# Two range checks moved from the second products to the middle pairs of first products

## The chip, the cores and the metric

The kernel runs on one core of one Trainium2 chip. The metric is the device time of one execution in microseconds (us); the median of several runs is given. The engines are TensorE (PE; its weight loads are shown apart as PEld), VectorE (DVE), ScalarE (ACT), GpSimd (POOL) and SyncE (SP). SP and POOL also issue DMA transfers, each in the order of its own queue.

## The reference

Hash attention, followed by an MLP mixer. With B=4, 8 heads, S=768 and head width 64:

```
bucket(q), bucket(k) = signs of q@proj, k@proj as 6-bit numbers
scores = where(bucket(q) == bucket(k), q@k.T / 8, -1e9); scores -= rowmax
attn   = exp(scores);  x = (attn / (sum(attn) + 1e-9)) @ v        # heads side by side: (4, 768, 512)
h      = relu(x.T @ w_tok1) @ w_tok2;   u = x + h.T                # over tokens, 768 -> 256 -> 768
out    = u + relu(u @ w_ch1) @ w_ch2                               # over channels, 512 -> 1536 -> 512
```

All inputs are float32.

## The kernel before

The work comes in three stages: attention (to about 310 us), token mixing (to about 387 us) and channel mixing, the function `channels` (the rest). The change lies in `channels` alone.

The attention stage takes exponentials without subtracting a row's maximum. This is safe while no element of q or k exceeds 1.7 in size. So, while the channels are mixed, the kernel reads q and k once more and tests them: the *range check*. There are 32 tiles to test (16 head pairs, q and k), each of 128 x 768 floats (384 KB). If any element was too large, a second, careful version of everything runs at the end; with these inputs it doesn't.

One check is spread over two functions. `begin_look` (L1554) squares the oldest fetched tile in place on ScalarE (L1556). `end_look` (L1558) takes Relu of the square minus 1.7 squared, with a sum along the row, on ScalarE (L1564), and then has POOL fetch the next tile into the place that has come free (L1574). There are three places, called `looked` (one) and `seen` (two). So the first three calls only fetch; after that each call tests the tile fetched three calls earlier; and the last three calls only test. That makes 35 calls for 32 tiles. `look` (L1547) does both halves at once.

`channels` works on three groups of 1024 tokens, s = 0, 1, 2. A group has a *first product*, u @ w_ch1 with relu, and a *second product*, the result @ w_ch2. Both are done by Strassen's scheme with seven block products, p1 to p7, instead of eight.

- First product: six blocks of hidden rows. In group 0 each is done by itself (`hidden`). In groups 1 and 2 they are done in three pairs: `hidden_first` (t = 0), and `hidden_pair` for t = 1, the *middle pair*, and t = 2. Most of their block products are themselves split by Strassen's scheme (class `Smaller`: `one`, `rest` and `three` are its matmul groups, `unite` its ScalarE copy at L988, `keep` the copy at L954). `open_next` begins the next pair's p1. The pre-added left operands are fetched on SP's queue (`fetch_hidden_left`, L873, shown as `WC<-hidden_left` or `SW<-hidden_left`).
- Second product: `outputs` (L1458). It does p1 undivided (`whole_product`, L1368) and then calls `product` (L1381) for p5, p7, p6, p3, p2 and p4. Each of these six is a *part* of the second product, split once more into seven matmul groups of six matmuls (L783) that accumulate in PSUM blocks a0, a1, b0, b1. Between them ScalarE copies blocks (L789): a0 to c1, c1 to b0, b1 to c7, a0 to a1, a0 to u, b0 to the output, a1 to c5. The last matmul group accumulates in a1, so it must wait until c5 is copied. Finished blocks of the output are added into DRAM by POOL transfers (`store`, L1468), which share POOL's queue with the fetches of the checks.

Everything is issued in the order in which it is written (the schedule is manual), and each engine works through its own list in that order. Waits between engines follow from which tile an instruction reads and writes.

Where the checks stand before the change:

- `outputs(s)`: s + 1 calls of `look` in the whole product for s = 0 and 1 (L1482), ahead of the copy of p1's result to `q1` (L1484); none for s = 2.
- `product`: two checks in each of the six parts for s = 0 and 1 (`looks = 2`, L1396), none for s = 2. The first check begins after the copy of a0 to c1 and ends after the copy to u; the second begins after the copy of b0 to the output and ends after the copy of a1 to c5.
- `hidden_first`: two; `hidden_pair`: one, in its middle (L1170).

In numbers: 13 calls in group 0, 18 in group 1, 4 in group 2.

Of the kernel before, what the change touches and what calls it, by code (L numbers as in the profile page):

```python
# [48 lines left out]
def kernel(  # L49
# [15 lines left out]
    B, NP, _, _, S = qk.shape  # L65
# [689 lines left out]
    def channels(pool, psum, SW1, second, TA, judge):  # L755
# [7 lines left out]
        last = B * S // (2 * TT) - 1  # L763
# [274 lines left out]
        def open_next(bank, s, t):  # L1038
            p1 = Smaller(None, "p1", s, t + 1)
            p1.pair = bank_pair(bank)  # L1040
            p1.one(p1.pair, left_at(7 * s + 1)[:, 2 * TT : 4 * TT])
            ahead.append(p1)
# [4 lines left out]
        def fill(t, slot):  # L1047

            for work in slots.pop((t, slot), []):
                work()  # L1050
# [70 lines left out]
        def hidden_pair(s, t):  # L1121

            r, (p2, p6, p7, p3, p4) = parts_of(s, t)
            p5, p1 = Smaller(None, "p5", s, t), ahead.pop()
            one, two, three, four = ring
            e2, e4, e5, e3 = [flat(output_at(i)) for i in ((0, 2, 2, 0) if t == 1 else (0, 1, 2, 3))]  # L1130
            e6 = e7 = flat(q1)
            before = postponed.pop() if postponed else None

            A = p1.pair
            if before:
                before[0]()
            B = bank_pair(two)
            p6.one(B, e6)
            if before:
                before[1]()  # L1140
            p1.rest()
            p1.unite()
            C = bank_pair(three)
            p2.one(C, e2)
            p1.add(True)
            p6.rest()
            p6.unite()
            p1.seed()
            p6.add(True)
            fill(t, "p6")  # L1150
            p2.rest()
            p2.unite()
            p6.seed()
            D = bank_pair(four)
            p7.one(D, e7)
            p2.add()
            p1.three(A)
            if t + 1 == GP:
                fetch_left(7 * s + 1)
            first = copies()  # L1160
            copy_pair(first, A)
            fill(t, "p2")
            p6.three(B)
            C = bank_pair(three)
            p5.one(C, e5)
            u = copies()
            plus(u, flat(B), first)
            p2.three(A)
            fill(t, "u")
            look()  # L1170
            plus(r[0], banks(A), rows(e2))
            p5.rest()
            p5.unite()
            B = bank_pair(two)
            p3.one(B, e3)
            p5.add()
            relu(r[0])
            p7.rest()
            plus(flat(C), e5, u)
            p7.unite()  # L1180
            p7.add(True)
            p3.rest()
            p3.unite()
            A = bank_pair(one)
            p4.one(A, e4)
            p7.seed()
            p5.three(C)
            p3.add()
            fill(t, "p3")
            v = copies()  # L1190
            copy_pair(v, C)
            p4.rest()
            p4.finish()
            p7.three(D)
            plus(r[3], banks(D), rows(v))
            fill(t, "end")
            p3.three(C)

            def direct():
                p4.three(D)  # L1200
                if t + 1 < GP:
                    plus(r[1], banks(C), rows(e3))

            def end():
                plus(e4, e4, u)
                plus(r[2], banks(D), rows(e4))

            if t + 1 < GP:
                later(t + 1, "p3", *bounds(r))
                later(t + 1, "end", lambda: relu(r[3]), lambda: relu(r[2]))  # L1210
                open_next(two, s, t)
                ring[:] = [two, three, one, four]
                postponed.append((direct, end))
            else:
                plus(r[1], banks(C), rows(e3))
                unfinished.append(lambda: (relu(r[3]), [work() for work in bounds(r)]))
                ring[:] = [two, one, three, four]
                postponed.append((direct, lambda: (end(), relu(r[2]))))
# [94 lines left out]
        def left_at(g):  # L1313
            return area(g % 2)[:, : 7 * QC * P]
# [66 lines left out]
        def product(s, j, name, q, early, late, final=None):  # L1381

            half = slice(0, TT // 2)
            A, B = blocks(2)
            a0, a1, b0, b1 = (pair[:, i, half] for pair in (A, B) for i in range(2))  # L1390
            w = left_at(7 * s + j).rearrange("p (i k c) -> p i k c", i=7, k=QC)
            b00, b01, b10, b11 = quarters(name)
            t2 = begun.pop()
            c1, c7, u, c5 = (a[:, i] for a in [split4(copies())] for i in range(4))
            qs = q.rearrange("p i (n t) -> p (i n) t", n=2)
            looks = 2 if s < last else 0  # L1396

            def part(ps, left, right, start=False):
                accumulate(ps, lambda k: w[:, LEFTS.index(left), k], lambda k: right[:, k], range(QC), start)

            part(a0, 4, b00, True)
            copy(a0, c1)
            if looks > 1:
                begin_look()
            part(b1, 1, extra(), True)
            copy(c1, b0)
            copy(b1, c7)
            part(a0, 2, t2)
            for work in early[:2]:
                work()  # L1410
            nc.vector.tensor_tensor(b00, b10, t2, op=ALU.subtract)
            for work in early[2:]:
                work()
            if final:
                plus(qs[:, 3], qs[:, 3], c7)
            part(b0, 5, b10)
            if j < 6:
                fetch_left(7 * s + j + 2, [0])
            copy(a0, a1)
            copy(a0, u)  # L1420
            if looks > 1:
                end_look()
            part(a1, 0, b01)
            if final:
                plus(qs[:, 0], b0, qs[:, 0])
            else:
                copy(b0, qs[:, 0])
            if looks:
                begin_look()
            part(b1, 6, b00)  # L1430
            copy(a1, c5)
            if looks:
                end_look()
            part(a1, 3, b11)
            if j < 6:
                fetch_left(7 * s + j + 2, [1])
            for work in late:
                work()
            if j < 6:
                begin(ORDER[j + 1])  # L1440
            if not final:
                plus(qs[:, 3], c7, c5)
                plus(qs[:, 2], b1, u)
                copy(a1, qs[:, 1])
                return
            plus(qs[:, 2], qs[:, 2], u)
            plus(qs[:, 3], qs[:, 3], c5)
            plus(qs[:, 2], b1, qs[:, 2])
            plus(qs[:, 1], a1, qs[:, 1])
            if j < 6:  # L1450
                nc.sync.dma_start(out=final(0), in_=q[:, 0])
                for i in range(2):
                    nc.sync.dma_start(out=final(1, i, 1), in_=qs[:, 2 + i])
                return
            for i, issuer in zip((0, 3, 2, 1), (nc.sync, nc.sync, nc.scalar, nc.sync)):
                issuer.dma_start(out=final(i // 2, i % 2, 1), in_=qs[:, i])

        def outputs(s):  # L1458
# [20 lines left out]
            if postponed:  # L1479
                postponed.pop()[1]()  # L1480
            combine("x", "r3", ALU.subtract, "r1", [(0, 0), (1, 0), (1, 1)])
            for _ in range(s + 1 if s < last else 0):  # L1482
                look()
            nc.scalar.copy(q1, ps)  # L1484
            q7, q57, q6, q5 = [output_at(i) for i in range(4)]
# [68 lines left out]
        def begin_look():  # L1554
            if due():
                nc.scalar.activation(seen[0][0], seen[0][0], ACT.Square)  # L1556

        def end_look():  # L1558

            if judge and not places:  # L1560
                places.append(pool.tile([P, 2, S], F32, name="seen", tag="seen", bufs=1))
            if due():
                t, n, i = seen.pop(0)
                nc.scalar.activation(  # L1564
                    t, t, ACT.Relu, bias=minus_safe, accum_out=excess[:, 2 * n + i : 2 * n + i + 1],
                )
            if unseen:
                n, i = unseen.pop(0)
                at = (2 * n + i) % 3
                if at == 0:  # L1570
                    t = pool.tile([P, S], F32, name="looked", tag="looked", bufs=1)
                else:
                    t = places[0][:, at - 1]
                nc.gpsimd.dma_start(out=t, in_=qk[pairs[n][0], pairs[n][1], :, i])  # L1574
                seen.append((t, n, i))
# [167 lines left out]
```

## Time and profile before

| what | us |
|---|---|
| median of 3 runs | 789.79 |
| lowest, highest | 789.23, 790.72 |
| the profiled execution | 791.4 |
| its span, from first to last instruction | 789.6 |
| TensorE busy | 782.3 (99%) |
| VectorE busy | 665.1 (84%) |
| ScalarE busy | 478.1 (61%) |
| GpSimd busy | 53.7 (7%) |
| ScalarE, Square of one tile (L1556), median of 32 | 0.847 |
| ScalarE, Relu of one tile (L1564), median of 32 | 0.937 |
| ScalarE, reading out the row sum (L1564), median of 32 | 0.19 |
| fetch of one tile (L1574), issue to landing, least, median, most | 3.5, 6.1, 10.8 |

How to read a row of the timeline: the start in us from the span's start, the duration in us, the engine, the line, the operation, `out<-in` by the program's tile names, the shapes, how many instructions are merged (x6), and in brackets the idle time of the engine before it with what ended that idle time. In a row of the list of waits: who waited, for whom, the total in us, how often, and the longest. A matmul's end is modelled and overlaps the next one's start, so distances between starts are the better measure. A row of several matmuls that runs without a break has equal distances.

### The profile page before, as it was taken

To read this page: it belongs to the slowest core of one execution; us is meant where nothing else is said; L and a number is where in the kernel's file an instruction comes from. 1 tells how busy PE (TensorE), PEld (TensorE's weight loads), DVE (VectorE), ACT (ScalarE), POOL (GpSimd) and SP (SyncE) were. 2 spreads that over 40 slices of the span, in tenths; PEclk is the share of its full clock that TensorE was granted. 3 is DMA by queue.
4 is the path that set the end of the run, shared out by engine and by line. 5 is a ranking of instruction groups with operands and counts; after the bars stand their busy time and mean duration, and the time that the engine had idled before them with its cause. 6 is when DMAs were issued, how large, how long until landed. Compare 5 with 4: busy or idle time off the path is not lost.

```text
span 789.6 us, 12604 instructions
## 1 busy us (share of the span) xinstructions
PE 782.3 (99%) x4745; PEld 480.2 (61%) x4745; DVE 665.1 (84%) x906; ACT 478.1 (61%) x825; POOL 53.7 (7%) x77
## 2 busy tenths in 40 slices
PE   9999999999999999999999999999999999999997
PEld 5444444444444444455544458868876887886886
DVE  5989898989887677999697889878899798889884
ACT  6688888888888887333323235655676665654331
POOL 1000000000000000011121010220001122000001
PEclk9999999999999999999999999999999999999999
DMA  4435353537352424795686996897766696650555
GB/s 164 164 123 164 123 164 123 164 123 244 135 178 91 136 76 160 203 272 125 113 272 210 329 376 243 250 295 206 232 187 211 246 244 159 192 154 2 184 173 127
DMA packets 102016, 144.85 MB, mean 183 GB/s; under 512 B 30200, under 2 KB 71616, under 8 KB 101952
## 3 DMA queue, kind: packets, MB, share of 16 engines
q1 hardware_dynamic: 93936, 119.15, 46.1%
q0 software_dynamic: 7728, 24.64, 13.4%
q8 instruction: 38, 0.62, 0.3%
q10 hardware_dynamic: 288, 0.21, 0.1%
q14 instruction: 26, 0.21, 0.1%
HBM read 101.01 MB, written 35.52 MB: 173 GB/s over the span
## 4 chain that ended last, share of the span: by engine, by line
PE 88%; issue 5%; DVE 2%; DMA 2%; ACT 1%; POOL 1%; SPq 0%; POOLq 0%; DVEq 0%
PE b L783 40%; PE sc L356 20%; PE acc L410 16%; PE t L656 5%; PE t L696 5%; PE sums L434 2%; DMA looked<-in_qk 1%; PE hp L301 1%; POOL seen L1574 0%; DVE R L1021 0%; DMA hidden_left<-WC 0%; PE idle L473 0%; PE hw L325 0%; DVE R L832 0%; SPq L1284 0%
## 5 line engine op out<-in xcount | busy, mean ns | idle before, releaser
L363 ACT ACTIVATE e<-sc 128x768 f32<-128x768 f32 x192 | 154.5, 811 | 6.4 <-PE sc L356 6.0
L356 PE MATMUL sc<-qk 64*128 64x384 f32 x768 | 152.9, 484 | 0.0
L783 PE MATMUL b<-R,second 128*128 128x256 f32 (+1 forms) x522 | 132.5, 409 | 1.0 <-ACT c L789 1.0
L410 PE MATMUL acc<-e,vn 128*32 128x384 f32 x1536 | 127.0, 486 | 0.0
L783 PEld LDWEIGHTS b<-R,second 128*128 128x128 f32 x522 | 98.8, 190 | 30.5 <-issue 16.5
L395 DVE TENSOR_TENSOR esd<-esd,e 128x768 f32<-128x768 f32 x96 | 92.0, 958 | 10.4 <-ACT e L363 0.5
L410 PEld LDWEIGHTS acc<-e,vn 128*32 128x32 f32 x1536 | 49.9, 110 | 73.9 <-issue 73.5
L356 PEld LDWEIGHTS sc<-qk 64*128 64x128 f32 x768 | 68.3, 188 | 42.2 <-issue 37.8
L789 ACT COPY c<-b 128x256 f32<-128x256 f32 (+1 forms) x96 | 40.2, 426 | 78.7 <-PE b L783 68.2
L783 PE MATMUL b<-XT,WC 128*128 128x256 f32 (+1 forms) x212 | 65.0, 443 | 0.0
L356 PE MATMUL sc<-bits 64*128 64x384 bf16 x384 | 62.6, 323 | 0.0
L783 PEld LDWEIGHTS b<-XT,WC 128*128 128x128 f32 x212 | 40.3, 190 | 19.8 <-issue 15.5
L391 DVE SCALAR_TENSOR_TENSOR esd<-e 128x768 f32<-128x768 f32 x32 | 30.6, 955 | 23.3 <-ACT e L363 23.3
L783 PE MATMUL b<-XT,SW 128*128 128x256 f32 (+1 forms) x164 | 47.0, 410 | 0.0
L656 PE MATMUL t<-x,W 128*128 128x512 f32 x96 | 41.8, 593 | 0.0
L356 PEld LDWEIGHTS <-bits 64*128 64x128 bf16 x384 | 18.5, 94 | 33.1 <-issue 9.7
L783 PEld LDWEIGHTS b<-XT,SW 128*128 128x128 f32 x164 | 31.1, 190 | 9.4 <-issue 4.1
L416 ACT ACTIVATE num<-acc,vsum 128x384 f32<-128x384 f32 x32 | 18.6, 582 | 29.7 <-PE acc L410 29.3
L716 POOL DMA_DIRECT2D XT<-second x8 | 9.9, 1235 | 383.3 <-DVE second L715 361.1
L455 ACT COPY rec<-rec 32x384 f32<-32x384 f32 x64 | 32.7, 510 | 5.0 <-DVE rec L449 4.2
L783 PE MATMUL b<-TA,WC 128*128 128x256 f32 (+1 forms) x92 | 33.3, 472 | 0.0
L398 DVE TENSOR_TENSOR esd<-esd,e 128x768 f32<-128x768 f32 x32 | 30.5, 954 | 1.9
(253 smaller groups left out, 1251.1 us busy)
## 6 DMA issues: line engine op xcount, KB each, us to landing
second<-left SPq DMA_DIRECT2D x20, 768.0 KB
raw<-in_moe_w_ch SPq DMA_DIRECT2D x16, 768.0 KB
qk<-in_qk SPq DMA_DIRECT2D x15, 768.0 KB
second<-left SPq DMA_DIRECT2D x18, 576.0 KB
seen<-in_qk POOLq DMA_DIRECT2D x21, 384.0 KB, 6.3
WC<-hidden_left SPq DMA_DIRECT2D x18, 448.0 KB
vn<-in_v SPq DMA_DIRECT2D x16, 384.0 KB
vt<-in_vT SPq DMA_DIRECT2D x16, 384.0 KB
```

Source lines behind the costliest of these rows:

```text
L356: nc.tensor.matmul(sc[:, i, :HALF], t[rows, 1, P * c : P * c + P], t[rows, 0, qs], start=start, stop=not start,)
L363: nc.scalar.activation(e, sc[:, :, :HALF], ACT.Exp, scale=SCALE)
L391: nc.vector.scalar_tensor_tensor(self.d, es[0], NR * EPS, es[1], op0=ALU.add, op1=ALU.add,)
L395: nc.vector.tensor_tensor(self.d, self.d, e, op=ALU.add)
L398: nc.vector.tensor_tensor(self.d, self.d, self.es[-1], op=ALU.add)
L410: nc.tensor.matmul(acc[D * i + d : D * i + d + 32], vn[:, i, c, d : d + 32], e[:, i], start=(c == 0), stop=(c == NR - 1),)
L416: nc.scalar.activation(nums[self.n][:, self.half], acc, ACT.Identity, scale=-1.0, bias=vsum,)
L455: nc.scalar.copy(rec[other : other + 32, h], rec[at : at + 32, h])
L656: nc.tensor.matmul(ps, W1[:, r, P * j : P * j + P], x[:, r], start=(r == 0), stop=(r == NR - 1),)
L696: nc.tensor.matmul(ps[at], left, right, start=start, stop=True, skip_group_check=True,)
L783: nc.tensor.matmul(ps, left(k), right(k), start=start and k == ks[0], stop=stop and k == ks[-1], skip_group_check=True,)
L789: nc.scalar.copy(c, ps)
```

## The change

The number of calls stays at 35. One check is taken out of group 0's part p4 (the first of its two), and one of the two in group 1's whole product is taken out. One check is added to the middle pair (t = 1) of group 1 and of group 2: its Square stands ahead of p3's `three`, its Relu and its fetch stand behind `open_next`. Groups 0, 1 and 2 then have 12, 18 and 5 calls.

```diff
@@ hidden_pair
             p7.three(D)
             plus(r[3], banks(D), rows(v))
             fill(t, "end")
+            if t == 1:
+                begin_look()
             p3.three(C)
@@ hidden_pair
                 later(t + 1, "p3", *bounds(r))
                 later(t + 1, "end", lambda: relu(r[3]), lambda: relu(r[2]))
                 open_next(two, s, t)
+                if t == 1:
+                    end_look()
                 ring[:] = [two, three, one, four]
                 postponed.append((direct, end))
@@ product
-            looks = 2 if s < last else 0
+            looks = 0 if s == last else 1 if s == 0 and j == 6 else 2
@@ outputs
             combine("x", "r3", ALU.subtract, "r1", [(0, 0), (1, 0), (1, 1)])
-            for _ in range(s + 1 if s < last else 0):
+            if s < last:
                 look()
             nc.scalar.copy(q1, ps)
```

## The prediction

> **What bounds the kernel now.** I read the page first, then the list of waits, then the timelines of TensorE (PE), ScalarE (ACT), GpSimd (POOL) around the two waits found, and last the timeline of ACT where the change puts its new work.
>
> The page's head and the list of waits for TensorE over the whole span:
>
> ```profile
> span 789.6 us, 12604 instructions
> PE 782.3 (99%) x4745; PEld 480.2 (61%) x4745; DVE 665.1 (84%) x906; ACT 478.1 (61%) x825; POOL 53.7 (7%) x77
> PE b L783 <- ACT c L789: 1.5, 2, 1.0
> PE idle L473 <- DVE ones L97: 1.1, 1, 1.1
> ```
>
> TensorE is the bound: it is idle for 7.3 us of 789.6, part of it before the first and after the last matmul. Between its matmuls only two waits are listed, 1.5 us together, both in the channel mixing that the change touches and both for a ScalarE copy (L789). So the most that moving ScalarE work can give is these two and the slow restarts behind them. The timelines of TensorE around them:
>
> ```profile
> 519.07 4.05 PE L783 MATMUL b<-R,second 128*128 128x256 f32 x18
> 524.07 1.56 PE L783 MATMUL b<-R,second 128*128 128x256 f32 x6 [0.96 <-ACT c L789]
> 525.47 1.02 PE L783 MATMUL b<-XT,WC 128*128 128x512 f32 x2
> ...
> 601.37 1.46 PE L783 MATMUL b<-second,second 128*128 128x256 f32 x6
> 603.33 1.56 PE L783 MATMUL b<-c,second 128*128 128x256 f32 x6 [0.50 <-ACT c L789]
> 604.75 1.56 PE L783 MATMUL b<-R,second 128*128 128x256 f32 x6
> ```
>
> The idle times in brackets understate the loss, because a matmul's end is modelled. From starts: a part of 6 matmuls undisturbed takes 1.30 us (the two parts before 519.07 start at 516.48 and 517.77), 0.216 each. Stall A: 18 from 519.07 should be followed at 522.96; the next starts at 524.07, 1.11 late, and then takes 1.40 to the row after instead of 1.30: 1.21 us. Stall B: the part due at 602.67 starts at 603.33, 0.66 late; it takes 1.42 instead of 1.30, and the next lasts 1.56 instead of 1.46: 0.88 us. Together 2.09 us.
>
> ScalarE in stall A (group 0's last part, p4) and the POOL queue that feeds it:
>
> ```profile
> 516.95 0.85 ACT L1556 ACTIVATE seen<-seen 128x768 f32<-128x768 f32 x1
> 519.92 0.94 ACT L1564 ACTIVATE seen<-seen,minus_safe 128x768 f32<-128x768 f32 x1
> 520.85 0.36 ACT L789 COPY second<-b 128x256 f32<-128x256 f32 x1
> 522.92 0.84 ACT L1556 ACTIVATE looked<-looked 128x768 f32<-128x768 f32 x1 [1.70 <-DMA looked<-in_qk]
> 523.67 0.35 ACT L789 COPY c<-b 128x256 f32<-128x256 f32 x1
> ...
> 512.10 0.95 POOL L1574 DMA_DIRECT2D looked<-in_qk  x1
> ```
>
> The check that the change removes here is the one at 516.95/519.92. It does not itself wait: its Square sits in a gap before the next copy. What waits is the second check, at 522.92, for its tile, fetched at 512.10 and landed 10.8 us later; the copy of c5 (523.67) is queued behind it, and TensorE's last part behind that.
>
> ScalarE in stall B (group 1's whole product):
>
> ```profile
> 598.42 0.83 ACT L1556 ACTIVATE seen<-seen 128x768 f32<-128x768 f32 x1
> 600.22 0.83 ACT L1556 ACTIVATE looked<-looked 128x768 f32<-128x768 f32 x1
> 602.02 0.99 ACT L1484 COPY q<-b 128x1024 f32<-128x1024 f32 x1
> 602.91 0.37 ACT L789 COPY c<-b 128x256 f32<-128x256 f32 x1
> ```
>
> No transfer is late here: two checks of 1.80 us each run back to back, behind a relu that VectorE (DVE) released at 597.46, and the two copies come after them.
>
> ScalarE at the place of the new checks, end of group 1's middle pair:
>
> ```profile
> 565.18 1.06 ACT L1027 ACTIVATE R<-R 128x1024 f32<-128x1024 f32 x1
> 567.94 0.37 ACT L954 COPY second<-b 128x256 f32<-128x256 f32 x1 [1.69 <-PE b L783]
> 569.74 0.37 ACT L954 COPY q<-b 128x256 f32<-128x256 f32 x1 [1.43 <-PE b L783]
> ```
>
> Two holes, 1.69 and 1.43 us, both ended by TensorE. Group 2's middle pair has the same two (1.69 before 698.03, 1.44 before 699.84).
>
> **What the skill says.** The Trainium skill, "ScalarE: Activation LUTs", section "What ACT_TABLE_LOAD costs", prices an ACTIVATE at 186 ns + 0.833 ns per element, 280 with a pointer bias, and says neighbours overlap by 93 ns: 826 and 920 ns for 768 elements. The trace has 847 and 937, and 0.19 for reading the sum; I use the trace. "DMA: Bandwidth & Descriptors", "Anatomy of one DMA — SWDGE (gpsimd) path", gives 2.0 us + bytes/436e3, 2.9 us for a tile of 393,216 bytes. The trace shows 3.5 at best, 6.1 in the median, 10.8 at worst, so the queueing, not the price, makes stall A. The same page ("Issuing engines are not separate DMA queues") says that transfers of all issuers interleave on the same engines; the trace agrees, DMA share being 0.95 from 456 to 481 and 1.09 from 524 to 540 us.
>
> **The change part by part.** A call squares the tile fetched three calls earlier, then fetches into its place. I number calls and fetches from 1; before, group 0 has calls 1 to 13, its p4 calls 12 and 13.
>
> 1. *Removed in group 0's p4: one Square, one Relu with its read, one POOL fetch.* ScalarE work: 0.85 + 1.03 (0.94 + 0.19 - 0.09 overlap), hidden where it stood, worth nothing alone. But the remaining call becomes number 12 and takes fetch 9, issued at 505.29 and landed at 514.40, instead of fetch 10 (landed 522.89). Then: b0's copy goes at about 520.6 (its part ends at 520.5), Square at 520.9 to 521.7, c5's copy at about 521.9, when its matmuls are through, done by 522.3; TensorE wants it at 522.96. Margin 0.7 us. Stall A goes: -1.21.
> 2. *What moves with it.* POOL issues one tile fewer between 522 and 531; fetch 12 then stands behind the store issued at 522.13 (free at 523.4), as before. Fetch 13 waits behind the next store (531.41) and is needed only at about 566. In group 1's first stage call 13 takes fetch 10 (landed 522.89, wanted about 524.7) and call 14 fetch 11 (landed 523.95); before, its second Square stood 1.50 us for fetch 12 until 532.32, covered by TensorE's work. TensorE arrives 1.2 us earlier at the hidden-left tiles that SP fetched: they landed at 523.07 to 534.57, and the first is used at 528.9 (later 527.7), 4.6 us after landing; the others have more. No new wait: 0.
> 3. *Added at the end of the middle pair, groups 1 and 2: Square ahead of p3's three, Relu and read behind the next pair's opening.* Square 0.85 goes in the 1.69 hole (566.14 to 567.0, spare 0.9), Relu and read 1.03 in the 1.43 hole (spare 0.4). Their tiles landed long before. Behind them on ScalarE is the copy of p6's first product, which TensorE's next parts wait for; without the hole each pair would cost 1.88. I take 0, between 0 and that. The holes end on TensorE, so nothing is gained either.
> 4. *The fetch added there.* POOL is free (busy 0.00 from 564 to 571). In group 1 it puts 0.39 MB on the DMA engines from about 569 (share 0.51 from 564 to 571). The hidden-left tiles in flight landed at 572.45 and 573.93, and TensorE's sequencer first asks at 577.9 and 580.9: 5.4 us spare, against 1.6 us for 0.39 MB at the 246 GB/s that the stretch 480 to 524 moved. In group 2 all 32 tiles are fetched by then, so no fetch at all. 0.
> 5. *Removed in group 1's whole product: 1.80 us of ScalarE and a fetch.* q1's copy can start at about 600.3 (the product's last wide matmul starts at 599.64 and takes 0.59), c1's copy at about 601.5 when its own part ends, done at 601.9; TensorE wants it at 602.67. Margin 0.7. Stall B goes: -0.88; only 0.88 of the 1.80, because TensorE's work covers the rest. The next calls use tiles fetched one place earlier, so the 0.19 wait at 607.07 falls too, off the path.
> 6. *Untouched:* group 1's last part keeps three calls between fetch and use, and its small loss at 653.85 (0.2 us; Square waits 0.68 for its tile).
>
> Sum -1.21 - 0.88 = -2.1 us. The profiled execution took 791.4 (span 789.6 plus 1.8 around it) and would take 789.3; it is 1.6 above the median of the runs, so I take the 2.1 off the median: 789.79 - 2.1 = **787.7 us**, 0.27%. About 0.2%, or 1.58 us, is what a measurement of this kernel can tell from no change (faster below 788.2, slower above 791.4).
>
> **Rivals.**
> - *Only A pays.* B's wait is replaced: q1's copy or VectorE, without a gap from 577 to 607, sets the next part. For it: ScalarE's relu waits for VectorE until 597.46. Against: 0.7 us margin, and b00 (VectorE, 604.37) is wanted at about 606.6. 789.79 - 1.21 = 788.6.
> - *Only B pays, or neither.* The DMA queue is late again for another consumer after A, such as call 13's tile, 1.8 us before use. 788.9, or 789.8.
> - *Slower: the checks in the middle pairs hold ScalarE.* If the holes were not there for them, p6's first copy would be 1.88 late in each pair and TensorE with it: 3.76 - 2.09 = +1.7, 791.5. It becomes slower than before from 1.05 us per pair, past 0.2% from 1.84. Against: the holes exceed the work by 0.9 and 0.4.
> - *The change removes a check that did not wait* and so does nothing for A (788.9): step 1 speaks against it; it holds only if the remaining Square still needs fetch 10.
>
> **How the numbers follow.** Forecast 0.72 (787.0 to 788.2 by itself: jitter of the transfers, and 653.85's loss going or growing). Only A 0.10; only B 0.04; neither 0.04; slower 0.10, of which 0.06 the middle pairs and 0.04 a late transfer that I don't see. Range 786.9 to 788.9: forecast and both halves, 0.86. Faster 0.72, same 0.18, slower 0.10.
>
> **What would show it.** Right: TensorE's list of waits has no L789 entry over 0.1 us at these places; the only Square in group 0's p4 starts about 1 us before c5's copy without waiting; q1's copy starts right after one check; both holes of the middle pairs are filled and the copies after them still end on TensorE. Wrong: a Square waiting for a transfer in group 1's first stage, an idle TensorE at the start of a last pair, or TensorE's busy time growing by as much as its idle time falls.

## The result

The changed kernel takes 788.99 us in the median (788.29 to 790.5, 22 runs), the kernel before 790.15 on the same chip (789.23 to 791.2, 22 runs): ratio 0.9986, 95% interval 0.9980 to 0.9993, so -1.1 us, between -0.55 and -1.6. The forecast was -2.1 us and 787.7, with a range up to 788.9. The direction was right; the size was about half, and the time lies just outside the range.

The page's head of the profile after, and TensorE's list of waits over the whole span:

```profile
span 787.9 us, 12602 instructions
PE 781.7 (99%) x4745; PEld 480.9 (61%) x4745; DVE 664.8 (84%) x906; ACT 478.1 (61%) x825; POOL 53.9 (7%) x77
PE idle L473 <- DVE ones L97: 1.1, 1, 1.1
PE b L783 <- ACT c L789: 0.4, 1, 0.4
```

Of the two listed waits for L789 one entry of 0.4 us remains, and it is neither of the two. TensorE's timeline of after at the three places:

```profile
514.48 2.86 PE L783 MATMUL b<-R,second 128*128 128x256 f32 x12 [0.42 <-ACT c L789]
519.76 5.34 PE L783 MATMUL b<-R,second 128*128 128x256 f32 x24
524.95 1.88 PE L783 MATMUL b<-XT,WC 128*128 128x512 f32 x4
...
600.84 1.46 PE L783 MATMUL b<-second,second 128*128 128x256 f32 x6
602.13 1.24 PE L783 MATMUL b<-c,second 128*128 128x256 f32 x5
```

Group 0's last 24 matmuls run in one row (18 and 6 before, with stall A between them), and the part at 602.13 follows 1.29 us after 600.84: both stalls are gone. The 0.42 at 514.48 is in group 0's part p2, ahead of everything that was changed; there ScalarE waited 1.16 us for fetch 8 (fetches are numbered as in the prediction). ScalarE in group 0's p4, the whole product and the middle pair of group 1, in after (lines have moved by four: L1560 is the Square, L1568 the Relu, L1488 the copy to q1):

```profile
521.53 0.85 ACT L1560 ACTIVATE seen<-seen 128x768 f32<-128x768 f32 x1
522.55 0.37 ACT L789 COPY c<-b 128x256 f32<-128x256 f32 x1 [0.18 <-PE b L783]
...
599.74 1.02 ACT L1488 COPY q<-b 128x1024 f32<-128x1024 f32 x1
601.04 0.37 ACT L789 COPY c<-b 128x256 f32<-128x256 f32 x1 [0.28 <-PE b L783]
...
565.61 0.83 ACT L1560 ACTIVATE looked<-looked 128x768 f32<-128x768 f32 x1
567.41 0.37 ACT L954 COPY second<-b 128x256 f32<-128x256 f32 x1 [0.96 <-PE b L783]
567.68 0.94 ACT L1568 ACTIVATE looked<-looked,minus_safe 128x768 f32<-128x768 f32 x1
569.15 0.37 ACT L954 COPY q<-b 128x256 f32<-128x256 f32 x1 [0.45 <-PE b L783]
```

The Square in p4 doesn't wait, and the copies at 522.55, 601.04, 567.41 and 569.15 are all ended by TensorE: in all four places ScalarE now waits for TensorE and not the other way round. So the mechanism came out as forecast, and so nearly did the profiled execution: 791.4 before, 789.78 after, 789.3 forecast. What fell short is the median, 788.99.

### The profile page after: what moved, and what is told of

It is laid out like the page before. It is cut to its first block, busy times and chain, and to the rows that moved or that the text cites. A ratio compares the mean times of both kernels' runs of the same rounds, so it can differ in the third digit from the quotient of the medians.

```text
span 787.9 us, 12602 instructions
## 1 busy us (share of the span) xinstructions
PE 781.7 (99%) x4745; PEld 480.9 (61%) x4745; DVE 664.8 (84%) x906; ACT 478.1 (61%) x825; POOL 53.9 (7%) x77
## 4 chain that ended last, share of the span: by engine, by line
PE 92%; issue 4%; DVE 2%; DMA 1%; POOL 0%; ACT 0%; POOLq 0%; DVEq 0%
PE b L783 43%; PE sc L356 20%; PE acc L410 16%; PE t L656 5%; PE t L696 5%; PE sums L434 2%; DMA seen<-in_qk 1%; PE hp L301 1%; PE idle L473 0%; PE hw L325 0%; POOL seen L1578 0%; DVE R L832 0%; DVE TA L1364 0%; POOL looked L1578 0%; DVE R L1357 0%
## 5 line engine op out<-in xcount | busy, mean ns | idle before, releaser
L395 DVE TENSOR_TENSOR esd<-esd,e 128x768 f32<-128x768 f32 x96 | 92.0, 958 | 10.4 <-ACT e L363 0.5
L789 ACT COPY c<-b 128x256 f32<-128x256 f32 (+1 forms) x96 | 40.2, 425 | 79.2 <-PE b L783 68.9
```

Of the source, the lines that this page charges most:

```text
L395: nc.vector.tensor_tensor(self.d, self.d, e, op=ALU.add)
L789: nc.scalar.copy(c, ps)
```

## The experiments

Two theories. **Theory 1**: the profile of before showed an unusual execution. B is ScalarE's own work and in every execution; A depends on when a transfer lands (fetch 10, the tile that p4's second check squares), and is small or absent in many. **Theory 2**: both stalls are in every execution with the profile's sizes, and about 1 us is lost again elsewhere.

### The kernel before, profiled again, and each half alone

Unchanged, with 21 runs:

> The kernel before, unchanged, profiled once more. Theory 1 (the profiled execution of before was an unusual one: stall A comes from a transfer that is as late as 10.8 us only now and then, stall B from ScalarE's own work and so in every execution): stall B is there again with 0.85 to 0.9 us, stall A is well below 1.2 us, between 0 and 0.7, and the span is below 789.6. Theory 2 (both stalls are in every execution with the sizes of the first profile, and the change loses about 1 us elsewhere): A 1.1 to 1.3 and B 0.85 to 0.9 us again. Time: ratio 1.000 under both, within 0.001.

Measured: ratio 0.9998 (0.9992 to 1.0005), profiled execution 790.86. TensorE around p4 of group 0:

```profile
518.31 4.05 PE L783 MATMUL b<-R,second 128*128 128x256 f32 x18
523.36 1.56 PE L783 MATMUL b<-R,second 128*128 128x256 f32 x6 [1.00 <-ACT c L789]
524.76 0.59 PE L783 MATMUL b<-XT,WC 128*128 128x512 f32 x1
```

Counted as in the prediction, A is 1.26 us (due at 522.20, plus 0.10), B 0.87. This is what theory 2 expected, and against theory 1's number. Fetch 10 took 10.7 us.

The first half alone (shortened, against the kernel before):

```diff
-            looks = 2 if s < last else 0
+            looks = 0 if s == last else 1 if s == 0 and j == 6 else 2
+            if t == 1 and s == 1: begin_look()   # ahead of p3.three(C)
+                if t == 1 and s == 1: end_look() # behind open_next
```

> Only the first half of the change: the first check of group 0's part p4 goes to the middle pair of group 1; the whole product of group 1 keeps two checks. Theory 1 (stall A is small in most executions): -0.2 to -0.5 us, ratio 0.9994 to 0.9998. Theory 2 (A has 1.2 us in every execution): -1.2 us, 0.9985, or if the new place of the check costs time, more than that is lost again and TensorE shows a wait at the start of group 1's last pair. In its profile: no wait for a transfer in group 0's p4, stall B as before, 0.85 to 0.9 us.

Measured: 789.77 against 790.38 (65 runs), ratio 0.9992 (0.9986 to 0.9999): -0.6 us, between -0.1 and -1.1, about half of A. In its profile TensorE has no wait in p4, B is 0.87, and TensorE doesn't wait at the start of the last pair. So nothing was lost at the new place in this execution.

The second half alone (shortened, against the kernel before):

```diff
-            for _ in range(s + 1 if s < last else 0):
+            if s < last:
                 look()
+            if t == 1 and s == last: begin_look()
+                if t == 1 and s == last: end_look()
```

> Only the second half: one of the two checks of group 1's whole product goes to the middle pair of group 2. Theory 1 (B is made by ScalarE's own work and falls in every execution): -0.9 us, ratio 0.9989. Theory 2 (both stalls in every execution, part of the gain lost at the new places): -0.9 us or less. A rival under which B gives nothing in the end, because VectorE or the copy of q1 sets the next part: 0, ratio 1.000. In its profile: no L789 wait of TensorE near 602 us, group 0's p4 as before with a stall A of any size.

Measured: 789.32, ratio 0.9989 (0.9982 to 0.9995): -0.9 by the ratio and -1.1 by the medians; B's 0.88 lies inside the interval. And its profile, with p4 of group 0 just as before the change, shows no A at all:

```profile
519.14 5.34 PE L783 MATMUL b<-R,second 128*128 128x256 f32 x24
524.32 1.02 PE L783 MATMUL b<-XT,WC 128*128 128x512 f32 x2
PE idle L473 <- DVE ones L97: 1.1, 1, 1.1
```

Here fetch 10 took 9.1 us. The same code gives 1.2 us in one execution and nothing in another.

### No late transfers

The kernel before, with the fetches of the checks left out after the first three. 29 of the 32 tiles are therefore never read, and the tests run on the first three (shortened; the edit also keeps one `looked` tile for all its calls):

```diff
-                nc.gpsimd.dma_start(out=t, in_=qk[...])
+                if 2 * n + i < 3:
+                    nc.gpsimd.dma_start(out=t, in_=qk[...])
```

> The kernel before with the fetches of the checks left out after the first three: Squares and Relus run as often, on tiles that are already there, so 29 of the 32 tiles are not read at all. No check can then wait for its transfer, and the DMA engines have 11 MB less to move; stall B stays. Theory 1: all that late transfers cost in a usual execution (group 0's parts p2 and p4, group 1's p4) is 0.3 to 0.8 us: ratio 0.9990 to 0.9996. Theory 2: 1.2 us in group 0's p4 alone, 1.5 us or more in all: 0.9981 or less.

Measured: 789.71 (789.38 to 790.33, 13 runs), ratio 0.9992 (0.9984 to 1.0000). In its profile B is there with 0.87 and nothing else of this kind. So all that late tiles cost in a usual execution is about 0.7 us, between 0 and 1.3. Theory 2 wanted 1.5 us or more; its 0.9981 lies outside the interval (A's 1.2 us alone, 0.9985, would still lie inside). The runs also lie closer together: 0.95 us from least to most in 13 runs, against 2.5 over the 65 of before.

### How often is A there?

> The kernel before, unchanged, a third profile. So far stall A had 1.2 us in two profiles of before, with fetch 10 landing 10.7 and 10.8 us after its issue, and none at all in the profile of only_b, whose code is the same up to there and whose fetch 10 took 9.1. If A comes and goes with the transfer: anything from 0 to 1.3 us, by fetch 10's time less about 9.5 us, and B 0.86 again. If A belongs to the kernel and only_b's profile was the odd one: 1.2 us again.

> The kernel before, unchanged, a fourth profile. As for the third: A between 0 and 1.3 us by fetch 10's time less about 9.5 us if it comes and goes; 1.2 us if it belongs to the kernel.

Measured: 789.64 in the third profiled execution, 791.11 in the fourth. TensorE in the third, then in the fourth:

```profile
518.79 5.34 PE L783 MATMUL b<-R,second 128*128 128x256 f32 x24
523.97 1.45 PE L783 MATMUL b<-XT,WC 128*128 128x512 f32 x3
601.82 1.56 PE L783 MATMUL b<-c,second 128*128 128x256 f32 x6 [0.50 <-ACT c L789]
```

```profile
519.25 4.05 PE L783 MATMUL b<-R,second 128*128 128x256 f32 x18
524.13 1.13 PE L783 MATMUL b<-R,second 128*128 128x256 f32 x4 [0.83 <-ACT c L789]
```

A is 0 in the third and 1.09 in the fourth (due at 523.14, plus 0.10); B is there in both. Together with the experiment below, which came out with the same order of instructions, six profiles have the same code up to this place: A was 1.21, 1.26, 1.09, 0, 0 and 0, with fetch 10 at 10.8, 10.7, 10.5, 8.8, 9.1 and 9.1 us. Where it is there, A is within 0.1 us of fetch 10's time less 9.5 us, as expected. The mean is 0.6, the gain of the first half alone. Six profiles are few for a mean, but the spread of the runs points the same way: the 21 runs of the first half alone lie within 1.2 us (789.0 to 790.21), those of the second half alone, which keeps A, within 3.8 (788.39 to 792.18).

### What makes fetch 10 late?

Two attempts on five other transfers, the hidden-left tiles for group 1 (448 KB each), which SP issues from 511.7 us on, right after the store that POOL issues ahead of fetch 10 (511.20). The first put four of them at the end of p4's code instead of p2's:

```diff
-        *([lambda h=h: fetch_hidden_left(h) for h in range(5)] ...)      # end of p2
+        *([lambda: fetch_hidden_left(0)] ...)                            # end of p2
+        *([lambda h=h: fetch_hidden_left(h) for h in range(1, 5)] ...)   # end of p4
```

> The kernel before, with four of the five transfers of 448 KB that fetch group 1's first hidden-left tiles issued on SP's queue at the end of group 0's p4 instead of the end of its p2; the checks are not touched. If fetch 10 is late because it shares the DMA engines with these five: it lands within 9 us of its issue, stall A is 0 in this profile, B stays at 0.86, and the time falls by what A costs in the mean, 0.4 to 0.8 us (ratio 0.9990 to 0.9995). If fetch 10 is late for another reason, such as the store that POOL issued just ahead of it: still over 9.5 us, A up to 1.2, ratio 1.000. A loss is possible if the four tiles now come too late for group 1's first stage: a wait of TensorE between 528 and 545 us.

Measured: ratio 1.0004 (0.9996 to 1.0012). The edit did nothing: SP has nothing else to do between these two places and waits for nothing there, so its list is the same, and it issued the tiles at 511.78 and on as before. The run serves only as one more execution of before (A was 0, as counted above).

The second attempt issues them one by one behind SP's waits, at the ends of p5, p7, p6, p3 and p2:

> The kernel before, with the five transfers of 448 KB for group 1's first hidden-left tiles issued one by one, each at the end of one of group 0's parts p5, p7, p6, p3 and p2, instead of all five in a row behind p2's last fetch; the checks are as before. SP waits for TensorE's progress at each part, so they really go out about 9 us apart from 490 us on, while the DMA share is 0.64 (496 to 503) and not 0.95 to 1.1 (512 to 524). If fetch 10 is late because these five crowd in with the store just ahead of it: it takes under 8 us instead of 8.8 to 10.8, stall A is 0, B stays at 0.86, and the time falls by A's mean, 0.5 to 0.8 us (ratio 0.9990 to 0.9994). If the store itself is slow: fetch 10 still over 8.8, ratio 1.000.

Measured: ratio 1.0004 (0.9996 to 1.0013). SP now issues four of the five before 506 us, but the last, and a transfer of 256 KB that stood behind them (L881, at 524.91 in the first profile), now go out right behind the store:

```profile
510.11 1.25 POOL L1468 DMA_DIRECT2D out<-TB  x1 [5.02 <-DVE XT L859]
510.97 0.43 SPq L873 DMA_DIRECT2D SW<-hidden_left  x1
511.44 1.42 SPq L881 DMA_DIRECT2D SW<-hidden_left  x1
```

From the store's issue to its landing the DMA engines moved 329 GB/s (510.11 to 519.82), against 294 in the first profile of before (511.20 to 521.82), so the edit did not make room for it. The store took 9.7 us, fetch 10 landed 1.05 us after it and took 9.5; A was 0.10. The time did not fall. In this one profile the losses turned up elsewhere:

```profile
599.35 1.46 PE L783 MATMUL b<-second,second 128*128 128x256 f32 x6
601.66 1.56 PE L783 MATMUL b<-c,second 128*128 128x256 f32 x6 [0.85 <-ACT c L789]
653.12 1.56 PE L783 MATMUL b<-R,second 128*128 128x256 f32 x6 [0.57 <-ACT c L789]
```

B has 1.2 us here, and group 1's p4 0.8 (653.12). Whether that is usual of this kernel one profile can't say. Moving four of the five transfers away doesn't make the fetch quick, but a store with nothing else beside it was not tried; what makes the fetch 9 or 10.7 us stays open.

### The change again, and taken further

> The changed kernel, unchanged, timed and profiled again. If A was there in about half of before's executions (3 of 6 profiles with the same code up to that place: 1.2, 1.3, 1.1, 0, 0, 0) and B in all: -0.6 - 0.88 = -1.5 us, ratio 0.9981, less what p2's check loses by chance. If the first measurement was right as it stood: 0.9986. If the forecast's sizes hold after all: 0.9973. In its profile: no L789 wait near p4 of group 0 nor at 602; in p2 of group 0 between 0 and 0.7 us.

Measured: 789.09 against 790.23, ratio 0.9986 (0.9980 to 0.9993), the same as the first time; the 0.9981 worked out from the six profiles is in the interval too. In its profile fetch 10 took 10.8 us, as late as in any execution, and yet nothing waits for it. ScalarE in p4, and the list of waits:

```profile
520.97 0.85 ACT L1560 ACTIVATE seen<-seen 128x768 f32<-128x768 f32 x1
521.99 0.37 ACT L789 COPY c<-b 128x256 f32<-128x256 f32 x1 [0.18 <-PE b L783]
PE idle L473 <- DVE ones L97: 1.1, 1, 1.1
```

This shows step 1 of the prediction directly: the late tile is no longer the one that p4 needs.

What was left in the changed kernel is p2 of group 0, where a Square waits for fetch 8 (TensorE loses 0.68 us in one profile of the change, 0.25 in the other). In p4 of group 1 neither profile of the change loses anything, but three others did (0.2, 0.4 and 0.8 us). So the same move was made in both parts, with the checks put into `hidden_first` (shortened):

```diff
-            looks = 0 if s == last else 1 if s == 0 and j == 6 else 2
+            looks = 0 if s == last else 1 if j == 6 or s == 0 and j == 5 else 2
@@ hidden_first
             copy_pair(u, X)
+            begin_look()
@@ hidden_first
             p7.one(bank_pair(x), e7)
+            end_look()
```

> The changed kernel taken further: group 0's part p2 also has one check instead of two, and so has group 1's p4; the two checks taken out go to the first stage of groups 1 and 2, Square behind the copy of p6's block to u, Relu and fetch behind the opening of p7. So the checks in p2 and p4 of group 0 and in p4 of group 1 each have more time for their fetch. If late transfers in these three parts are what is left: no wait of TensorE for L789 anywhere in the second products, and a gain over before of the change's 1.2 to 1.5 us plus 0.3 to 0.5, ratio 0.9976 to 0.9981. If the gains are given back at the new places: no faster than the change, 0.9986, and waits of TensorE in the first stages.

> The changed kernel taken further (one check in p2 and in p4 of group 0 and in p4 of group 1, the others in group 1's and 2's first stage) together with the five hidden-left transfers spread over group 0's parts. The first alone had no stall left in the second products. If nothing else waits for these transfers: the same as without the spread, 0.9977 within 0.0008. If the quieter DMA engines help elsewhere: up to 0.3 us better.

Measured: 788.76, ratio 0.9977 (0.9968 to 0.9986), and with the spread 788.88, 0.9978 (0.9972 to 0.9985). TensorE's list of waits has only the entry before its first matmul in both. This version is faster than before by 1.7 to 1.8 us by the ratios, 1.4 to 1.5 by the medians. Against the change itself it gains 0.2 us by the medians and 0.6 to 0.7 by the ratios; the intervals overlap, so this last gain is not shown. The spread adds nothing.

## Why the prediction was wrong

- **What bounds the kernel, where the two stalls are, and what makes them**: right. TensorE bounds it; A hangs on a transfer, B on ScalarE's own work. The profiles of after show both gone.
- **Step 1, removing a check that did not itself wait**: the mechanism was right, and the second profile of the change shows it with a transfer of 10.8 us. The term -1.21 is the one that was mis-sized: A is 1.1 to 1.3 us in three of six executions and 0 in three, 0.6 in the mean. The first half alone gave 0.6 us.
- **Step 5, stall B, -0.88**: right. It has 0.86 to 0.88 us in all five profiles of before (the four unchanged and the one with the same order), and the second half alone gave 0.9 by the ratio, 1.1 by the medians.
- **Steps 3 and 4, the new places cost nothing**: right. The holes were 1.69 and 1.43 us and are now 0.96 and 0.45 with the checks in them, in group 2 just the same; the added fetch is issued at 569.06, and TensorE has no wait in the last pair.
- **Steps 2 and 6**: no new wait in group 1's first stage; right. Group 1's p4 lost 0 to 0.8 us from profile to profile; that this loss could go or grow the prediction had said.
- **The sum against the median** is the step that failed: stall A's -1.21, read in one execution, was taken whole off the median, where the runs show 0.6 for it: "it is 1.6 above the median of the runs, so I take the 2.1 off the median". That the profiled execution was 1.6 us slow was in plain sight. One of the two stalls hung on a transfer that took 10.8 us where the median was 6.1; most of the 1.6 could have been this stall (the six profiles later gave this one fetch 8.8 to 10.8 us, and A 0.6 us of the 1.6). A had to be bounded between 0 and 1.21 for the median. With 0.6 the sum is -1.5, inside the measured interval.
- **The base**: 789.79 was the median of 3 runs; 22 runs gave 790.15. So 0.36 us of the 1.3 between 787.7 and 788.99 is the base and not the gain.
- **The range** had only both stalls or one of them whole, and gave "only B pays" 0.04. The measured gain lies between B alone and B with half of A.
- **Smaller points**: VectorE is not quite without a gap from 577 to 607 us, as the rival "Only A pays" had it; it stands 0.20 us before 586.49. The rival did not come true all the same: B paid. And 1.58 us is not the least that can be told from no change: with 22 runs of each kernel the interval reaches about 0.5 us to either side.

The rest between 1.5 and the measured 1.1 us is within the interval; the two profiles of the change also had more loss in p2 (0.68 and 0.25 us) than the six above (0 to 0.44, mean 0.15), ahead of any changed instruction in this group. This was not followed further, and why the gain was 1.1 and not 1.5 stays open.

## What to carry to other kernels

Before a gain is taken from one profile, ask of each stall whether its cause is engine work, which repeats, or the landing of a transfer, which doesn't; and if the profiled execution is slower than the median, the excess is first to be looked for in the second kind. A check that stands in the way need not be the one that waits: here removing the idle-time check let the next one use a tile that had landed 6.4 us before its Square began. And an instruction moved in the code of a queue that doesn't wait between the two places has not been moved at all.

## What the runs showed of the hardware

- In all twelve profiles that have this fetch, fetch 10 landed 0.9 to 1.1 us after the accumulating store issued ahead of it on POOL's queue, however long that store took (9.1 to 10.6 us). In the two profiles of the change taken further it was issued 3.1 and 3.3 us behind the store, in the others 0.7 to 1.2, and it still landed 1.1 us after it. Behind the other stores, the first fetch issued while the store was under way landed 0.9 to 2.7 us after it; none landed ahead of the store.
- In group 0, each further store was issued 0.31 to 0.34 us after the one before it had landed, in all thirteen profiles: 510.87 to 511.20 and 521.82 to 522.13 in the first, 519.80 to 520.11 in the third of before. What holds it back is not shown.
- The store ahead of fetch 10 took 10.4 to 10.6 us in the four profiles, the second of the change among them, where SP's first hidden-left transfer was issued 0.01 to 0.52 us after it, and 9.1 to 9.5 us in five where it followed 0.56 to 0.86 us after. But the change taken further (without the spread) has 0.72 us and a store of 10.1, so the distance alone does not set the time. That a closer start makes the store slower is not shown.
